# A planned dense stage is planned anew: other durations, a shared port between two engines, new priorities, and one DRAIN

## The chip, the core and the metric

The kernel runs on one core of a Trainium2 chip. A core has five engines with instruction queues of their own, each executed in order: TensorE (PE in the profile; PEld is its weight load), VectorE (DVE), ScalarE (ACT), GpSimd (POOL) and SyncE (SP), which issues most of the DMAs. They wait for each other by semaphores. The metric is the time of one execution on the device, in microseconds (us).

## The reference

Three layers over 4608 tokens (8 sequences of 576, 8 heads of 64). Everything is float32.

```python
kv = einsum('bhsd,bhse->bhde', k, v); out = einsum('bhsd,bhde->bhse', q, kv)
x = out / sqrt(mean(out*out, -1) + 1e-6) * g_norm            # attention without softmax; x is [4608, 512]

h = x @ w_in                                                 # dense layer: [512, 2048]
x = (h * clip(h + 3, 0, 6) / 6) @ w_out                      # [2048, 512]

out = x.copy()                                               # experts
xc = x[x @ w_skip > 0]; logits = xc @ w_gate                 # 8 experts, one for each token
e_idx = argmax(logits, 1); gate_w = softmax(logits)[e_idx]
y[mask_e] = gate_w * (maximum(xc[mask_e] @ w1[e], 0) @ w2[e])    # w1 [512, 1024], w2 [1024, 512]
out[x @ w_skip > 0] = xc + y
```

## The kernel before

**Products.** Every large product is made of three: each operand is split into a high part (rounded to the fp32r type) and a low part (what is left), and high x high, high x low and low x high are added in PSUM. Each split is a copy on ScalarE and a subtraction on VectorE or GpSimd.

**Dense stage.** Attention goes by 16 units `u` of 288 tokens and 4 head pairs `p`: `K` (k by v, fp32, from a load `kv` of 512 KB and one of 64 KB), `K2` and `K2m` (a mask on its result, VectorE), `A` (q by kv), `A2` (square), `B` (sum over a head), `B2l`, `B2`, `N`, `N2a`, `N2b`, `N2` (the norm), `Xh` and `Xl` (the split of x, which is the dense layer's input). The dense layer goes by 18 chunks `c` of 256 tokens and 16 blocks `f` of 128 of the 2048 columns: `G1` (12 matmuls into the PSUM tile `h`), `g` 1 to 4 (relu, product `t`, high part `gh`, low part `gl`), `G2` (6 matmuls into `y`). `route` then computes nine dot products a 128-token tile (`dot`), picks the expert and scatters the token's number into the table `tab` by an indirect DMA of GpSimd.

**Weights.** w_in and w_out come as 64-bit floats. `convert` turns each of 32 pieces (512 columns on 128 partitions; even numbers from w_in, odd ones from w_out) into float32 and splits it: `c1` to `c4` on VectorE (lines 600, 604, 607, 611), `sg` (line 615, a sum) on either engine, `h` on ScalarE, `l` (line 621, the low part) on either engine. Four staging places `SG` are used in turn. Chunks 0 and 1 are computed while the weights are being converted.

**What sets the order.** All these are `op`s: name, engine, a duration in us, the function that emits it, what it depends on, and tokens for buffers that it takes and gives. `Plan.order` goes through them as a list scheduler: at each moment every free engine takes the ready op with the highest priority (the longest chain behind it plus `BIAS` of its `kind`), and engine `VP` means VectorE or GpSimd, whichever takes it first, 2.05 times as long on GpSimd. The instructions are then emitted in the order of the planned starts. On the chip each engine goes through its list in order and waits where a dependency is late.

**Experts.** After the dense stage come 8 blocks of experts, written out by hand (`block`, `V128`), with side work in 10 steps of each block (`sd[0]` to `sd[9]`). GpSimd gathers the rows of an expert's tokens (`rows<-y_scr,idx`) and scatters the results (`final<-rows,idx`) by indirect DMAs. The next expert's counts are loaded in step 6 (`begin`); the last expert has none to load.

Of the kernel before, what the change touches and what calls it, by code (L numbers as in the profile page):

```python
# [28 lines left out]
    "t": 1, "g": 3, "row": 4, "rt": 2,  # L29
}  # L30
BIAS = {
# [11 lines left out]
    ("scat", 0): -250, ("scat", 1): -64, ("slot", 0): 104, ("slot", 1): -17, ("y", 0): -52, ("y", 1): -175,  # L43
    ("yd", 0): -90, ("yd", 1): 12, "bump": -172, "bump2": -190, "cp": -23, "fT": -185, "fTh": -7, "fTl": -165,
    "ixc": -50, "late h": 112, "late l": -40, "rowsc": -110, "wh": 14, "wl": -248, "wlo": 41, "z": -31,
    "zero": 250,
}
BIG = 1.0e6


class Plan:

# [11 lines left out]
    @staticmethod  # L64
    def kind(name):
        if isinstance(name, str):
            return name
        k, n = name[0], name[1]
        if k == "c":
            return ("ld" if name[2] == "ld" else "c", n // 8)  # L70
        if k in ("kv", "K", "K2", "K2m", "K2h"):
            return (k[0:1] if k[0] == "K" else k, min(n // 4, 2) + (n >= 12))
        if k[0] in "ABNX" or k in ("q", "qh", "ql"):
            return (k if k[0] == "q" else "A" if k[0] == "B" else k[0], min(n, 3) + (n >= 6))
        if k == "g":
            return ("g", name[3] + 4 * (n > 1) + 4 * (n > 3))
        if k in ("G1", "G2"):
            return (k, min(n, 2) + (n >= 4))
        if k in ("dot", "pick", "exp", "rank", "slot", "scat"):
            return (k, int(n >= 8))  # L80
        if k in ("y", "yd"):
            return (k, int(n >= 4))
        return k

    def add(self, name, eng, cost, fn, deps=(), take=(), give=(), dma=0.0, bonus=0.0):
        self.ops.append((name, eng, cost, fn, tuple(deps), tuple(take), tuple(give), dma, bonus))

    def order(self):
        ops = self.ops
# [21 lines left out]
        left = [len(p) for p in preds]  # L111
        done, start = {}, {}
        wait = {e: [] for e in self.ENGINES}
        giving, t, dma_free, n_left = [], 0.0, 0.0, len(ops)

        def add_wait(i):
            eng = ops[i][1]
# [10 lines left out]
        while n_left:  # L128
            keep, nxt = [], []
            for g in giving:  # L130
                if g[0] <= t + 1e-9:
                    self.free[g[1]] += 1
                else:
                    keep.append(g)
                    nxt.append(g[0])
            giving = keep
            for e in self.ENGINES:
                if busy[e] > t + 1e-9:
                    nxt.append(busy[e])
                    continue  # L140
                best = None
                for w in wait[e]:
                    if w[1] in start:
                        continue
                    if w[2] > t + 1e-9:
                        nxt.append(w[2])
                    elif best is None or w < best:
                        take = ops[w[1]][5]
                        if all(self.free[k] >= take.count(k) for k in take):
                            best = w  # L150
                if best is None:
                    continue
                i = best[1]
                _, eng, cost, _, _, take, give, dma, _ = ops[i]
                wait[e] = [w for w in wait[e] if w[1] not in start and w[1] != i]
                for k in take:
                    self.free[k] -= 1
                start[i] = t
                fin = busy[e] = t + (cost * 2.05 if eng == "VP" and e == "P" else cost)
                if e == "S":  # L160
                    dma_free = max(fin + self.DMA_ISSUE, dma_free) + dma
                    fin = dma_free + self.DMA_LAT
                else:
                    fin += dma
                done[i] = (fin, e)
                giving += [(fin + self.LAT * (e != "-"), k) for k in give]
                nxt += [busy[e], fin, t + 1e-6 if e == "-" else fin]
                n_left -= 1
                for j in succs[i]:
                    left[j] -= 1  # L170
                    if not left[j]:
                        add_wait(j)
                        nxt.append(t + 1e-6)
            if n_left:
                nxt = [x for x in nxt if x > t + 1e-9]
                assert nxt, [o[0] for i, o in enumerate(ops) if i not in start and not left[i]]
                t = min(nxt)
# [5 lines left out]
def fused_kernel(ctx, tc, qT, kvm, kvr, gv, w_in, w_out, w9, w9t, w1, w2, cst, tokid, out):  # L183
# [107 lines left out]
    def st_K(j):  # L291
        def mm(_):
            t = kv_t.pop(j)
            if j < 4:
                ps = ps_h.tile([128, 128], F32, tag="h", name="kvp")
            else:
                ps = ps_o.tile([128, 128], F32, tag="o", name="kvp")
            for i in range(5):
                n = 128 if i < 4 else 64
                nc.tensor.matmul(ps, t[0:n, 0, i, :], t[0:n, 1, i, :], start=(i == 0), stop=(i == 4))  # L300
            kvp_t[j] = ps

        op(("K", j), "PE", 2.1 if j < 3 else 1.07, mm, [("kv", j)] + [("y", 1, 1)] * (j >= 8), take=[k_tok(j)], give=["kv"] if j >= 8 else [])

    def st_K2(j):
        def km0(_):
# [59 lines left out]
    def st_A(u, p):  # L366
# [20 lines left out]
        op(("A", u, p), "PE", 0.48 if u < 2 else 0.36, mm, deps, take=[a_tok(u, p)],  # L387
           give=["qs", "qs"] * (u >= 2) + ["kh"] * (u % 2) + ["kl"] * (u % 2 and u > 2))

    def st_A2(u, p):  # L390
# [23 lines left out]
    def st_B(u, p):  # L414
# [8 lines left out]
            m_t[u, p] = m  # L423

        if u < 3:
            op(("B", u, p), "PE", 0.48, mm, [("A2", u, p)], take=[b_tok(u, p)])
        else:
            op(("B", u, p), "PE", 0.24, mm, [("A2l", u, p)], take=[b_tok(u, p)], give=["ss", "ss"])

    def st_B2(u, p):  # L430
        def ln(_):
# [43 lines left out]
    def st_N2(u, p):  # L475
# [13 lines left out]
        op(("N2a", u, p), "V", 0.37, f1, [("N", u, p)], give=[b_tok(u, p)])  # L489
        op(("N2b", u, p), "V", 0.43, f2, [("N", u, p), "consts"], give=[a_tok(u, p)])  # L490
        op(("N2", u, p), "V", 0.37, f3, [("N2a", u, p), ("N2b", u, p)], give=["a"] if u >= 3 else [])

    def st_X(u, p):
        parts, done = [], 0
# [179 lines left out]
    def G1(c, f):  # L674
# [11 lines left out]
            deps.append("late l")  # L686
        if f == 0 and c >= 2:
            deps += [("G1", c - 1, 15)] if c > 2 else [("G1", 0, 15), ("G1", 1, 15)]
        op(("G1", c, f), "PE", 1.31, mm, deps, take=["h"], bonus=1.28)

    h_t = {}

    def G1e(c, f):
# [23 lines left out]
            g_t[c, f] = (gh, gl)  # L717

        tk = "a" if second else "t"
        op(("g", c, f, 1), "A", 0.36, relu, [("G1", c, f)], take=[tk])  # L720
        op(("g", c, f, 2), "V", 0.34, mul, [("g", c, f, 1)], give=["h"])
        op(("g", c, f, 3), "A", 0.31, high, [("g", c, f, 2)], take=["g"])
        op(("g", c, f, 4), "VP", 0.34, low, [("g", c, f, 3)], give=[tk])

    def G2(c, f):
        def mm(_):
# [8 lines left out]
            mm3([(y_t[c][i], (gh[:, t], gl[:, t]), (wh[:, f % 4, :], wl[:, f % 4, :])) for i, t in enumerate(ts)], f == 0, f == 15)  # L735

        deps = [("w", ("out", f // 4), f % 4), ("g", c, f, 4)] + ([("G2", c, f - 1)] if f else [])
        op(("G2", c, f), "PE", 1.29, mm, deps, take=[] if f else ["y", "oy" if c == 1 else "y"],
           give=["g"], bonus=1.28)

    ysb = {}
# [66 lines left out]
    def route(i):  # L808

        for j in range(9):  # L810
            op(("dot", i, j), "V", 0.62, lambda _, j=j: rt_dot(i, j, j + 1), [("y", i // 2, i % 2), "w9"] + ([("dot", i, j - 1)] if j else [("dot", i - 1, 8)] if i else []),
               take=["rt"] if j == 0 else [])
        op(("pick", i), "V", 0.7, lambda _: rt_pick(i), [("dot", i, 8), ("cp", 1), ("cp", 2), ("cp", 3)], give=["row"])
        op(("exp", i), "A", 0.25, lambda _: rt_exp(i), [("pick", i)])
# [338 lines left out]
    for k in range(NE):  # L1153
# [100 lines left out]
```

## Time and profile before

| what | value |
|---|---|
| median of 3 runs | 1327.14 us (1323.95 to 1329.03) |
| the profiled execution's own time | 1326.83 us |
| its span, first to last instruction | 1325.1 us |
| mean granted TensorE clock | 0.982 |
| busy share of the span | PE 95%, DVE 68%, ACT 46%, POOL 28% |

The span is what the trace covers; the execution's own time is 1.7 us longer. A busy share is a mean over stages that differ: the first 185 us (attention of the first tokens, conversion of the weights, chunks 0 and 1), the rest of the dense stage up to about 897 us, the experts up to about 1312 us, and the end. The granted clock is a share of 2.4 GHz; 0.5 is the lower of its two levels, 1.2 GHz. Busy time on VectorE and GpSimd runs from an instruction's start to its end and may hold time in which it was held up.

### The profile page before, as it was taken

The page shows a single profiled execution, that of the slowest core. Times are in us where ns is not written, and L with a number is a line of the kernel's source. Part 1 is how long each engine was busy: PE and PEld are TensorE (multiplying, and loading weights), DVE is VectorE, ACT ScalarE, POOL GpSimd, SP SyncE. Part 2 cuts the span into 40 slices and gives each one's busy share as a digit, 9 for nine tenths or more (in the row PEclk, how much of TensorE's full clock was granted, in tenths as well). Part 3 has the DMA queues.
Part 4 walks back from the last instruction along what each step waited for, and adds up shares of the span by engine and source line. Part 5 has one row for each costly group of instructions (what it writes and reads, how often), then busy time and mean ns, then how long its engine had stood idle before and what let it go on. Part 6 is the DMA issues. An engine that isn't in the chain of part 4 may idle for free. (4 is left out here: it accounts for less than half of the span.)

```text
span 1325.1 us, 22326 instructions
## 1 busy us (share of the span) xinstructions
PE 1254.8 (95%) x7857; PEld 1120.5 (85%) x7857; DVE 899.0 (68%) x2435; ACT 603.3 (46%) x1514; POOL 376.1 (28%) x399
## 2 busy tenths in 40 slices
PE   5787799999999999999999999999999999999995
PEld 4676688898888998989989999998988888889885
DVE  4999989758778458768667767677675266555431
ACT  2543354535654334555554554563353255344320
POOL 2756744414331013122122122130043122223111
PEclk9798999999999999999999999999999999999998
DMA  9333343202111201121121121100146055555300
GB/s 300 101 111 112 96 167 100 77 1 82 51 19 55 86 1 46 59 68 46 42 68 59 47 68 42 47 5 33 65 143 187 32 188 168 164 180 165 127 25 24
DMA packets 77632, 114.48 MB, mean 86 GB/s; under 512 B 17158, under 2 KB 38550, under 8 KB 77360
## 3 DMA queue, kind: packets, MB, share of 16 engines
q1 hardware_dynamic: 70944, 98.12, 23.6%
q0 software_dynamic: 6544, 14.58, 3.4%
q8 instruction: 73, 1.20, 0.4%
q14 instruction: 71, 0.58, 0.2%
HBM read 91.25 MB, written 26.05 MB: 89 GB/s over the span
## 5 line engine op out<-in xcount | busy, mean ns | idle before, releaser
L768 DVE CUSTOM_DVE_ANT_0 junk<-ysb,w9b 128x512 bf16<-128x512 f32 x306 | 226.2, 739 | 4.9 <-ACT ysb L747 2.3
L701 ACT ACTIVATE t<-h,half 128x256 f32<-128x256 f32 x288 | 136.2, 474 | 205.0 <-PE h L665 103.5
L716 POOL TENSOR_TENSOR gl<-t,gh 128x256 fp32r<-128x256 f32 x120 | 103.3, 861 | 317.6 <-ACT gh L710 214.0
L710 ACT ACTIVATE gh<-t 128x256 fp32r<-128x256 f32 x288 | 119.5, 415 | 156.5 <-DVE t L706 104.7
L706 DVE SCALAR_TENSOR_TENSOR t<-t,h 128x256 f32<-128x256 f32 x288 | 119.8, 417 | 73.6 <-ACT t L701 71.8
L656 PE MATMUL y<-wh,gh 128*128 128x512 f32 x400 | 131.4, 403 | 1.2 <-ACT gh L710 1.1
L656 PE MATMUL y<-wl,gh 128*128 128x512 f32 x400 | 128.0, 394 | 1.7 <-DVE wl L621 1.7
L656 PE MATMUL y<-wh,gl 128*128 128x512 f32 x400 | 126.8, 392 | 0.1
L656 PE MATMUL y<-WH,gh 128*128 128x512 f32 x384 | 126.2, 404 | 0.0
L656 PE MATMUL y<-WH,gl 128*128 128x512 f32 x384 | 121.6, 392 | 3.6 <-DVE gl L716 3.6
L716 DVE TENSOR_TENSOR gl<-t,gh 128x256 fp32r<-128x256 f32 x168 | 81.2, 484 | 63.4 <-PE y L656 31.8
L656 PE MATMUL y<-WL,gh 128*128 128x512 f32 x384 | 122.1, 394 | 0.0
L665 PE MATMUL h<-x12h,wh 128*128 128x256 f32 x576 | 94.7, 287 | 15.2 <-DVE t L706 13.2
L665 PEld LDWEIGHTS h<-x12h,wh 128*128 128x128 f32 x576 | 84.4, 190 | 26.8 <-DVE t L706 17.1
L958 DVE SCALAR_TENSOR_TENSOR gl<-h,gh 128x256 fp32r<-128x256 f32 x88 | 37.3, 423 | 98.6 <-ACT gh L957 96.3
L957 ACT ACTIVATE gh<-h 128x256 fp32r<-128x256 f32 x88 | 33.8, 384 | 143.9 <-PE h L665 127.7
L665 PE MATMUL h<-x12h,wl 128*128 128x256 f32 x576 | 93.5, 285 | 0.0
L665 PE MATMUL h<-x12l,wh 128*128 128x256 f32 x576 | 93.4, 285 | 0.0
L656 PEld LDWEIGHTS y<-wl,gh 128*128 128x128 f32 x400 | 75.5, 189 | 20.0 <-DVE wl L621 2.6
L656 PEld LDWEIGHTS y<-wh,gl 128*128 128x128 f32 x400 | 75.4, 189 | 17.7 <-DVE gl L716 0.6
L656 PEld LDWEIGHTS y<-WH,gl 128*128 128x128 f32 x384 | 72.4, 189 | 20.5 <-DVE gl L716 4.5
L656 PEld LDWEIGHTS y<-WL,gh 128*128 128x128 f32 x384 | 72.7, 189 | 16.5
(205 smaller groups left out, 2722.1 us busy)
## 6 DMA issues: line engine op xcount, KB each, us to landing
kv<-kvm SPq DMA_DIRECT2D x24, 512.0 KB
stgh<-w SPq DMA_DIRECT2D x22, 512.0 KB
stgl<-w SPq DMA_DIRECT2D x21, 512.0 KB
stg<-w SPq DMA_DIRECT2D x21, 512.0 KB
y_scr<-ysb SPq DMA_DIRECT2D x36, 256.0 KB
final<-ysb SPq DMA_DIRECT2D x36, 256.0 KB
SG<-w_in SPq DMA_DIRECT2D x16, 512.0 KB
SG<-w_out SPq DMA_DIRECT2D x16, 512.0 KB
```

What stands on the lines that cost most here:

```text
L656: nc.tensor.matmul(ps, st[a], mv[b], start=first and (a, b) == (0, 0) and all(p[0] is not ps for p in prods[:q]), stop=last and (a, b) == ...
L665: nc.tensor.matmul(ps, st[a], mv[b], start=first and (a, b) == (0, 0) and all(p[0] is not ps for p in prods[:q]), stop=last and (a, b) == ...
L701: nc.scalar.activation(t, h_t[c, f], ACTF.Relu, bias=half, scale=1.0 / 6.0)
L706: nc.vector.scalar_tensor_tensor(t, t, 1.0, h_t.pop((c, f)), op0=ALU.min, op1=ALU.mult)
L710: nc.scalar.activation(gh, g_t[c, f], ACTF.Copy)
L716: eng_of[e].tensor_tensor(gl, t, f32(gh), op=ALU.subtract)
L768: nc.vector.tensor_tensor_reduce(junk, ysb[i], W9["t"][:, j, :], 1.0, 0.0, ALU.mult, ALU.add, accum_out=lg[:, j:j + 1])
L957: nc.scalar.activation(gh, ps, ACTF.Relu)
L958: nc.vector.scalar_tensor_tensor(gl, ps, 0.0, f32(gh), op0=ALU.max, op1=ALU.subtract)
```

## The change

The planner gets other durations (G1 from 1.31 to 1.44 us, G2 from 1.29 to 1.385, and smaller ones of the same kind), finer kinds, and with them a new table BIAS of 154 priorities. In the planner, an instruction on GpSimd and one on VectorE of the kinds that `alone` names no longer run at the same time: the later one begins when the `port` is free. At the end, the last expert's step 6 gets a DRAIN of GpSimd.

```diff
@@ BIAS (one line of 17 each)
-    ("c", 0): 40, ("c", 1): 18, ("c", 2): -117, ("c", 3): -140, ("dot", 0): 140, ("dot", 1): 61,
+    ("c", 1): 48, ("c", 2): -83, ("c", 3): 54, ("c", 4): -439, ("c", 5): 36, ("c", 6): -97, ("c", 7): -179,
...
@@ kind
         if k == "c":
-            return ("ld" if name[2] == "ld" else "c", n // 8)
+            if name[2] == "ld":
+                return ("ld", n // 2 if n < 16 else n // 4 + 4)
+            return ("cl" if name[2] in ("sg", "l") else "c", n // 4)
...
+    @staticmethod
+    def alone(name, eng):
+        if eng == "VP":
+            return True
+        return eng == "V" and not (name[0] in ("K2", "K2m", "N2a", "N2b", "slot", "fTl") or (name[0] == "g" and name[3] == 2))
+
@@ order
-                fin = busy[e] = t + (cost * 2.05 if eng == "VP" and e == "P" else cost)
+                if eng == "VP" and e == "P":
+                    cost = 2.05 * cost + 0.07
+                begin = t
+                if e in ("V", "P") and self.alone(ops[i][0], eng):
+                    begin = max(t, port)
+                    port = begin + cost - (0.2 if e == "P" else 0)
+                fin = busy[e] = begin + cost
...
-        op(("G1", c, f), "PE", 1.31, mm, deps, take=["h"], bonus=1.28)
+        op(("G1", c, f), "PE", 1.44, mm, deps, take=["h"], bonus=1.28)
...
-        op(("G2", c, f), "PE", 1.29, mm, deps, take=[] if f else ["y", "oy" if c == 1 else "y"],
+        op(("G2", c, f), "PE", 1.385, mm, deps, take=[] if f else ["y", "oy" if c == 1 else "y"],
...
@@ the loop over experts
         if k + 1 < NE:
             sd[6].append(lambda: begin(k + 1))
+        else:
+            sd[6].append(nc.gpsimd.drain)
```

What the new plan emits differs from the first instruction on. The lines of the changed kernel are 22 or 24 higher: 622, 626, 629, 633 are c1 to c4 (before 600, 604, 607, 611), 637 and 643 the sum and the low part (615, 621), 322 is K (300), 398 A of the first two units (376), 441 B (419), 687 G1 (665). `sh` and `sl` are places in the weights' buffers that hold kv, q and the norm's tiles while the weights are not there yet.

SP, from its first instruction. Before (`kvm` and `kvr` are the loads of k and v, `cst` constants, `SG` a conversion's staging place):

```order
L272 DMA sh_107<-kvm 128x2x512
L273 DMA sh_107<-kvr 64x2x128
L272 DMA sh_108<-kvm 128x2x512
L273 DMA sh_108<-kvr 64x2x128
L272 DMA sh_109<-kvm 128x2x512
L273 DMA sh_109<-kvr 64x2x128
L1040 DMA sh_106<-cst 128x128
L285 DMA sl_110<-qT 128x288 x4
L272 DMA sh_106<-kvm 128x2x512
L273 DMA sh_106<-kvr 64x2x128
L1039 DMA sh_106<-cst 128x272
L637 DMA SG<-w_in 128x4x256
```

(ahead of these stand one more pair of kvm and kvr). With the change:

```order
L659 DMA SG<-w_in 128x4x256 x2
L659 DMA SG<-w_out 128x1024
L1062 DMA sh_106<-cst 128x128
L659 DMA SG<-w_out 128x1024
L307 DMA sl_110<-qT 128x288 x4
L1061 DMA sh_106<-cst 128x272
L294 DMA sh_106<-kvm 128x2x512
L295 DMA sh_106<-kvr 64x2x128
L294 DMA sh_107<-kvm 128x2x512
L295 DMA sh_107<-kvr 64x2x128
L294 DMA sh_108<-kvm 128x2x512
L295 DMA sh_108<-kvr 64x2x128
```

Four conversion loads now stand ahead of the first load of k and v; before, five such pairs, two loads of constants and four of q stood ahead of the first conversion load.

VectorE, from the fifth instruction on (four memsets stand ahead in both; `km` is K2, `sl<-o` and `sl<-m` are N2b and N2a, `x0l` and `x12l` the low parts of x). Before:

```order
L1041 CAST boR<-sh_106 128x128
L308 TENSOR_TENSOR km_165<-kvp,boR 128x128
L308 TENSOR_TENSOR km_167<-kvp,boR 128x128
L1043 TENSOR_SCALAR g_sb<-g_sb 128x1
L308 TENSOR_TENSOR km_188<-kvp,boR 128x128
L308 TENSOR_TENSOR km_194<-kvp,boR 128x128
L600 TENSOR_SCALAR wbits<-SG 128x512
L604 SCALAR_TENSOR_TENSOR wbits<-SG,wbits 128x512
L607 TENSOR_SCALAR SG<-wbits 128x512
L611 SCALAR_TENSOR_TENSOR SG<-SG 128x512
L615 TENSOR_TENSOR wbits<-wbits,SG 128x512
L600 TENSOR_SCALAR wbits<-SG 128x512
```

With the change:

```order
L622 TENSOR_SCALAR wbits<-SG 128x512
L626 SCALAR_TENSOR_TENSOR wbits<-SG,wbits 128x512
L629 TENSOR_SCALAR SG<-wbits 128x512
L622 TENSOR_SCALAR wbits<-SG 128x512
L633 SCALAR_TENSOR_TENSOR SG<-SG 128x512
L626 SCALAR_TENSOR_TENSOR wbits<-SG,wbits 128x512
L622 TENSOR_SCALAR wbits<-SG 128x512
L1063 CAST boR<-sh_106 128x128
L629 TENSOR_SCALAR SG<-wbits 128x512
L1065 TENSOR_SCALAR g_sb<-g_sb 128x1
L622 TENSOR_SCALAR wbits<-SG 128x512
L633 SCALAR_TENSOR_TENSOR SG<-SG 128x512
```

The first conversion stood behind the four K2, and now stands first. In the order of VectorE's instructions the first c1 is at place 11 before and 5 now, the last low part of a weight at 258 and 260.

TensorE, up to its first dense matmuls. Before, it began with four K (rows not shown), then:

```order
L376 MATMUL o_192<-sl_110,km_165 128x288
L376 MATMUL o_196<-sl_110,km_167 128x288
L376 MATMUL o_201<-sl_110,km_188 128x288
L376 MATMUL o<-sl_110,km_194 128x288
L419 MATMUL m<-sl_112,boR 128x288 x2
L376 MATMUL o_235<-sl_111,km_167 128x288
L376 MATMUL o_240<-sl_111,km_194 128x288
L419 MATMUL m<-sl_112,boR 128x288 x2
L376 MATMUL o<-sl_111,km_165 128x288
L300 MATMUL kvp<-sh_106 128x128 x5
L419 MATMUL m<-sl_112,boR 128x288 x2
L665 MATMUL h<-x0h,WH 128x256 x4
```

With the change, behind six K, six A and three B:

```order
L441 MATMUL m<-sl_112,boR 128x288 x2
L322 MATMUL kvp<-sh_108 128x128 x5
L398 MATMUL o<-sl_110,km_262 128x288
L322 MATMUL kvp<-sh_109 128x128 x5
L441 MATMUL m<-sl_112,boR 128x288
L398 MATMUL o<-sl_111,km_225 128x288
L441 MATMUL m<-sl_112,boR 128x288
L687 MATMUL h<-x0h,WH 128x256 x4
```

The first `h` stood behind five K and came before the A of unit 1's third pair; now it stands behind eight K, all eight A of units 0 and 1 and seven of their eight B. The low part of x that it needs is at place 38 of VectorE's order before and 96 now.

Over the whole dense stage the choice between VectorE and GpSimd moves 69 instructions to GpSimd, 44 of them the low parts `gl` (line 716): 120 of 288 on GpSimd before, 164 now.

## Rows read from the trace of the kernel before

**Rows 1.** The page, part 1: busy us (share of the span) xinstructions.

```profile
PE 1254.8 (95%) x7857; PEld 1120.5 (85%) x7857; DVE 899.0 (68%) x2435; ACT 603.3 (46%) x1514; POOL 376.1 (28%) x399
```

**Rows 2.** Table by stages: stretch, its length, busy us (xinstructions) by engine, PEclk, DMA share, GB/s.

```profile
0.00:18.50 18.50, 11.32 (x41) 9.39 (x42) 1.50 (x10) 1.28 (x1) 1.51 (x6) 1.00 0.86 269
36.00:185.00 149.00, 117.96 (x648) 99.86 (x646) 145.82 (x224) 64.56 (x157) 94.90 (x80) 0.90 0.34 100
245.00:897.00 652.00, 649.23 (x4203) 588.18 (x4202) 459.92 (x1471) 332.34 (x880) 158.35 (x190) 1.00 0.16 48
897.00:1312.00 415.00, 407.19 (x2560) 363.61 (x2558) 222.50 (x520) 162.56 (x358) 87.97 (x86) 1.00 0.37 119
```

**Rows 3.** Timeline, PE, 35 to 37 us: start, us, instruction.

```profile
36.06 0.85 PE L665 MATMUL h<-x0h,WH 128*128 128x256 f32 x4
```

**Rows 4.** Waits of PE, 36 to 185 us: total, times, longest us.

```profile
PE h L665 <- DVE t L706: 21.7, 16, 3.4
```

**Rows 5.** Timeline, DVE, 18.4 to 21.6 us.

```profile
18.54 0.42 DVE L600 TENSOR_SCALAR wbits<-SG 128x512 int32<-128x512 int32 x1
19.00 0.69 DVE L604 SCALAR_TENSOR_TENSOR wbits<-SG,wbits 128x512 int32<-128x512 int32 x1
```

**Rows 6.** Groups of DVE, 18.5 to 185 us: busy us, mean ns | idle before.

```profile
L604 DVE SCALAR_TENSOR_TENSOR wbits<-SG,wbits 128x512 int32<-128x512 int32 x32 | 31.7, 995 | 0.1
L611 DVE SCALAR_TENSOR_TENSOR SG<-SG 128x512 f32<-128x512 uint32 x32 | 29.7, 932 | 0.1
L607 DVE TENSOR_SCALAR SG<-wbits 128x512 int32<-128x512 int32 x32 | 25.2, 793 | 0.1
L600 DVE TENSOR_SCALAR wbits<-SG 128x512 int32<-128x512 int32 x32 | 18.7, 584 | 0.0
L482 DVE SCALAR_TENSOR_TENSOR sl<-o,g_sb,sl 128x288 f32<-128x288 f32 x12 | 5.9, 510 | 2.5 <-ACT sl L470 2.4
```

**Rows 7.** Timeline, DVE and POOL, 98 to 100.6 us.

```profile
98.62 1.66 POOL L615 TENSOR_TENSOR wbits<-wbits,SG 128x512 f32<-128x512 f32 x1 [0.63 <-DVE SG L611]
99.06 1.43 DVE L515 TENSOR_TENSOR x12l<-sl,x12h 128x192 fp32r<-128x192 f32 x1
```

**Rows 8.** Timeline, DVE, 181 to 187 us.

```profile
183.09 1.50 DVE L621 TENSOR_TENSOR wl<-wbits,wh 128x512 fp32r<-128x512 f32 x1 [0.28 <-ACT wh L618]
```

**Rows 9.** Timeline, POOL, 1288 to 1313 us.

```profile
1289.12 0.98 POOL L934 DMA_INDIRECT final<-rows,idx  x1 [21.96 <-DVE rows L933]
...
1312.64 1.01 POOL L934 DMA_INDIRECT final<-rows,idx  x1 [0.34 <-DVEq L1196]
```

**Rows 10.** Line 1250, the end of the program: min/median/max ns, first and last start us.

```profile
L1250 POOLq DRAIN  x3: 46/109/8646, 1315.6 to 1324.8; - x3
```

**Rows 11.** Timeline, SP and PE, 0 to 6 us.

```profile
0.75 0.69 SPq L272 DMA_DIRECT2D sh<-kvm  x1
5.05 1.22 PE L300 MATMUL kvp<-sh 128*128 128x128 f32 x4 [5.05 <-DMA sh<-kvm]
```

**Rows 12.** Table, 36 to 185 us, of instructions on tile h, then on tile y.

```profile
36.00:185.00 149.00, 64.04 (x408) 59.35 (x408) 12.94 (x33) 15.21 (x33) 0.90 0.34 100
36.00:185.00 149.00, 47.12 (x174) 33.10 (x174) 0.00 (x0) 0.00 (x0) 0.90 0.34 100
```

**Rows 13.** Groups of DVE and POOL, 245 to 897 us.

```profile
L716 DVE TENSOR_TENSOR gl<-t,gh 128x256 fp32r<-128x256 f32 x129 | 58.6, 454 | 57.2 <-PE y L656 31.8 <-ACT gh L710 25.4
L716 POOL TENSOR_TENSOR gl<-t,gh 128x256 fp32r<-128x256 f32 x79 | 64.8, 820 | 292.7 <-ACT gh L710 195.9 <-PE pr L838 60.7 <-issue 25.9
```

**Rows 14.** DMA issues of POOL's queue, indirect.

```profile
rows<-y_scr,idx POOLq DMA_INDIRECT x38
tab<-pay,slot POOLq DMA_INDIRECT x36
final<-rows,idx POOLq DMA_INDIRECT x26
```

More of the change, by code (lines that the diff above doesn't have):

```diff
@@ L31 @@
 BIAS = {
[11 rows of a table removed]
[L43 to L46, printed above, removed]
[9 rows of a table added]
+    ("cl", 7): 216, ("dot", 0): -165, ("dot", 1): -278, ("exp", 0): 197, ("exp", 1): 139, ("g", 1): 195,
[6 rows of a table added]
+    ("ql", 3): -174, ("ql", 4): 62, ("rank", 0): 182, ("rank", 1): -20, ("scat", 0): 110, ("scat", 1): -260,
+    ("slot", 0): -206, ("slot", 1): -57, ("y", 0): 118, ("y", 1): -153, ("yd", 0): -155, ("yd", 1): -97,
+    "bo": 100, "bump": 200, "bump2": 189, "consts": -44, "cp": 10, "cs": -161, "cs1": -84, "fT": 234, "fTh": -118,
+    "fTl": 232, "g": -240, "ixc": 201, "late h": -33, "late l": 136, "rowsc": 101, "swap": -23, "tab": -241,
+    "tok": -95, "w": 98, "w9": 37, "wh": -287, "wl": -132, "wlo": 202, "z": -116, "zero": -26,
 }
@@ L69, in kind @@
         if k == "c":
-            return ("ld" if name[2] == "ld" else "c", n // 8)
+            if name[2] == "ld":
+                return ("ld", n // 2 if n < 16 else n // 4 + 4)
+            return ("cl" if name[2] in ("sg", "l") else "c", n // 4)
         if k in ("kv", "K", "K2", "K2m", "K2h"):
-            return (k[0:1] if k[0] == "K" else k, min(n // 4, 2) + (n >= 12))
+            return (k, min(n // 4, 2) + (n >= 12))
         if k[0] in "ABNX" or k in ("q", "qh", "ql"):
-            return (k if k[0] == "q" else "A" if k[0] == "B" else k[0], min(n, 3) + (n >= 6))
+            return (k if k in ("q", "qh", "ql", "A2l", "Xl") else "A" if k[0] == "B" else k[0], min(n, 3) + (n >= 6))
         if k == "g":
@@ L113, in order @@
         wait = {e: [] for e in self.ENGINES}
-        giving, t, dma_free, n_left = [], 0.0, 0.0, len(ops)
+        giving, t, dma_free, port, n_left = [], 0.0, 0.0, 0.0, len(ops)
         def add_wait(i):
@@ L301, in mm @@
             kvp_t[j] = ps
-        op(("K", j), "PE", 2.1 if j < 3 else 1.07, mm, [("kv", j)] + [("y", 1, 1)] * (j >= 8), take=[k_tok(j)], give=["kv"] if j >= 8 else [])
+        op(("K", j), "PE", 2.1 if j < 3 else 1.12, mm, [("kv", j)] + [("y", 1, 1)] * (j >= 8), take=[k_tok(j)], give=["kv"] if j >= 8 else [])
     def st_K2(j):
@@ L386, in st_A @@
             deps.append(("G1", u * UN // CH - 3, 15))
-        op(("A", u, p), "PE", 0.48 if u < 2 else 0.36, mm, deps, take=[a_tok(u, p)],
+        op(("A", u, p), "PE", 0.52 if u < 2 else 0.4, mm, deps, take=[a_tok(u, p)],
            give=["qs", "qs"] * (u >= 2) + ["kh"] * (u % 2) + ["kl"] * (u % 2 and u > 2))
@@ L425, in st_B @@
         if u < 3:
-            op(("B", u, p), "PE", 0.48, mm, [("A2", u, p)], take=[b_tok(u, p)])
+            op(("B", u, p), "PE", 0.5, mm, [("A2", u, p)], take=[b_tok(u, p)])
         else:
-            op(("B", u, p), "PE", 0.24, mm, [("A2l", u, p)], take=[b_tok(u, p)], give=["ss", "ss"])
+            op(("B", u, p), "PE", 0.27, mm, [("A2l", u, p)], take=[b_tok(u, p)], give=["ss", "ss"])
     def st_B2(u, p):
@@ L487, in f3 @@
             r_t[u, p] = r
-        op(("N2a", u, p), "V", 0.37, f1, [("N", u, p)], give=[b_tok(u, p)])
-        op(("N2b", u, p), "V", 0.43, f2, [("N", u, p), "consts"], give=[a_tok(u, p)])
-        op(("N2", u, p), "V", 0.37, f3, [("N2a", u, p), ("N2b", u, p)], give=["a"] if u >= 3 else [])
+        op(("N2a", u, p), "V", 0.4, f1, [("N", u, p)], give=[b_tok(u, p)])
+        op(("N2b", u, p), "V", 0.4, f2, [("N", u, p), "consts"], give=[a_tok(u, p)])
+        op(("N2", u, p), "V", 0.4, f3, [("N2a", u, p), ("N2b", u, p)], give=["a"] if u >= 3 else [])
     def st_X(u, p):
@@ L719, in G1e @@
         tk = "a" if second else "t"
-        op(("g", c, f, 1), "A", 0.36, relu, [("G1", c, f)], take=[tk])
-        op(("g", c, f, 2), "V", 0.34, mul, [("g", c, f, 1)], give=["h"])
-        op(("g", c, f, 3), "A", 0.31, high, [("g", c, f, 2)], take=["g"])
+        op(("g", c, f, 1), "A", 0.385, relu, [("G1", c, f)], take=[tk])
+        op(("g", c, f, 2), "V", 0.334, mul, [("g", c, f, 1)], give=["h"])
+        op(("g", c, f, 3), "A", 0.33, high, [("g", c, f, 2)], take=["g"])
         op(("g", c, f, 4), "VP", 0.34, low, [("g", c, f, 3)], give=[tk])
@@ L810, in route @@
         for j in range(9):
-            op(("dot", i, j), "V", 0.62, lambda _, j=j: rt_dot(i, j, j + 1), [("y", i // 2, i % 2), "w9"] + ([("dot", i, j - 1)] if j else [("dot", i - 1, 8)] if i else []),
+            op(("dot", i, j), "V", 0.69, lambda _, j=j: rt_dot(i, j, j + 1), [("y", i // 2, i % 2), "w9"] + ([("dot", i, j - 1)] if j else [("dot", i - 1, 8)] if i else []),
                take=["rt"] if j == 0 else [])
```

24 rows, old and new, of the table BIAS are left out of this document.

## The prediction

> **What bounds the kernel now.** I read the totals first: TensorE is busy 95% of the span [rows 1], so only its idle time can be won. The table by stages says where that lies [rows 2]. From 245 to 897 us TensorE idles 652.0 - 649.2 = 2.8 us, in the expert stage 415.0 - 407.2 = 7.8 us. What is left is the beginning and the end: from 36 us (the first matmul of the dense layer, 36.06 us [rows 3]) to 185 us TensorE works 118.0 of 149 us at a mean granted clock of 0.90, before that it has little to do, and in the last 14 us it does nothing.
>
> In the beginning the reader is to see VectorE: 145.8 of 149 us busy, GpSimd 94.9 us. TensorE's main wait there is for the tile t, a VectorE product (21.7 us in 16 waits [rows 4]). VectorE is late because it converts w_in and w_out: 32 conversions of four instructions each (c1 to c4) and two subtractions or sums (c5, low) that either engine takes. Alone, c1 takes 0.42 and c2 0.69 us [rows 5]; c3 and c4 are the same two kinds on the same 128x512 tile, so 2.22 us for a conversion. In the stage their means are 0.584, 0.995, 0.793 and 0.932 us, 105.3 us in all against 32 x 2.22 = 71.0 us alone: 34 us of VectorE's "busy" time is waiting [rows 6]. For whom, the timeline shows: a GpSimd sum runs from 98.62 to 100.28 us, and a VectorE subtraction of 192 columns that starts at 99.06 us ends at 100.49 us [rows 7], 1.43 us for 192 columns, where c2 takes 0.69 for 512. An instruction that reads PSUM (L482, mean 0.510 us) shows no such stretch [rows 6]. So what ends this stage is the two engines' work taken one after the other, and it begins when VectorE begins to convert, at 18.54 us [rows 5], and ends with the last low, 183.09 + 1.50 = 184.6 us [rows 8].
>
> At the end, the last scatter is issued at 1312.64 us [rows 9], and a DRAIN of GpSimd that begins at 1315.6 us takes 8.646 us of the 12.5 us that are left; the shortest DRAIN of that line took 0.046 us [rows 10].
>
> **The change, part by part.** The sum is made against the profiled execution, 1326.8 us, which is 0.3 us under the median of 1327.14.
>
> *The start of the conversions.* SP now issues two loads of w_in before anything else, then w_out; the kv loads come after four conversion loads, four of q and two of constants. Before, the first 512 KB load was issued at 0.75 us and its user ran at 5.05 us, 4.3 us later [rows 11]. By the same 4.3 us the first conversion can start at 5.1 instead of 18.54 us: 13.4 us earlier. What stands on VectorE from the first conversion to the last low is nearly the same: places 11 to 258 of its order before, 5 to 260 now, with 32 of each of c1 to c4 and 10 sums on VectorE in both; 9 subtractions before the last one then, 10 now; GpSimd has 22 sums and 22 subtractions, now 22 and 21. The eight more places are the six small instructions (boR, four km, g_sb) that stood ahead of the first conversion, and two others. Before, 247 places took 183.09 - 18.54 = 164.6 us, 0.666 us each, waits included. Now 255 places would take 170 us: the last low starts at 175 us and ends at 176.5, 8 us earlier. Counted by work alone (the six small ones take some 1.5 us, not 4) it would end at 5.1 + 164.6 + 1.5 + 1.5 = 172.7 us, 12 us earlier. Waits for the delayed kv are in the way: up to the first kv 3.5 MB stand in the queue, at the 269 GB/s of the first 18.5 us [rows 2] that is 13 us, and the four K took TensorE's 11.3 us of work up to 18.5 us. VectorE comes to its first km (place 20) at 15 us, so a wait of 1 to 3 us. I take 10 us. Bounds: nothing (all given back to waits), and 25 us, if the 34 us of waiting [rows 6] shrink by a third as well.
>
> *What comes after.* At the last low both orders have as much of chunks 0 and 1 behind them (14 and 14 second matmuls then, 15 and 15 now), and chunk 2 has just begun. From 245 us on TensorE is full [rows 2], so what is won in the beginning stays won, unless waits take it back there.
>
> *TensorE begins later.* The first matmul of chunk 0 now needs the fourth head pair's x, whose last part stands at place 96 of VectorE's order: 5.1 + 91 x 0.666 + 2 = 68 us instead of 36. The stage's matmuls into h and y are 64.0 + 47.1 = 111 us busy at clock 0.90 [rows 12], about 100 at the full clock that the next stages show. 68 + 100 to 111 = 168 to 179 us: with 10 to 11 conversions in stock TensorE can run without gaps, and would end about with VectorE. So this costs nothing as long as TensorE works nearly all the time.
>
> *More subtractions on GpSimd.* In the whole dense stage 44 of the 288 gl (128x256) move to GpSimd (120 before, 164 now). From 245 to 897 us one takes 0.820 us there and 0.454 us on VectorE [rows 13]. GpSimd is busy 158.4 of 652 us there, VectorE 459.9 [rows 2], and TensorE waits 2.8 us for everything: I take nothing. If that cover were gone, 44 x 0.366 = 16 us. The GPSIMD Engine Reference of the Trainium skill (4.1, Engine selection) speaks against this part: an elementwise operation with two inputs belongs on VectorE, GpSimd takes about twice the time. The rows agree (0.820 / 0.454 = 1.8); by that rule alone the forecast would be 16 us longer, 1325 us.
>
> *The other edits of the planner* (durations, finer kinds) act through the order alone. The end of the dense stage (first experts' weights, the first gather) is planned nearly as before; taken at nothing, with 3 us to either side.
>
> *The DRAIN.* In the last expert GpSimd gets one more DRAIN, behind the scatters of the expert before and ahead of its own. There GpSimd waits 21.96 us for VectorE before the scatter at 1289.12 us [rows 9], so 8.65 us more are hidden, and nothing else is queued behind it. What it does to the last DRAIN no row shows. Lower bound: it removes nothing, the long one stays. Upper bound: the last one becomes as short as the shortest, 8.6 us. Before the long one GpSimd had issued 38 + 36 + 26 indirect transfers [rows 14] and five plain ones; after the new one there are six first and last of six in [rows 9]. If a DRAIN's time goes with what was issued since the last one, the last would take 8.65 x 6 / 105 = 0.5 us. I take 8 us, since the two DRAINs that follow closely on the long one are the nearest rows, and they are short.
>
> Sum: 1326.8 - 10 - 8 = **1309 us**.
>
> **The rivals.** *The drain does nothing*: 1326.8 - 10 = 1317. For it: no row has a DRAIN after few transfers. Against: all transfers had landed when it began, so it does not wait for data.
> *The earlier start is given back*: kv, and with it x, come later, VectorE stands behind them in its fixed order, and the last low comes at 183 to 186 us; with the drain 1319. For it: three of the four km stand between conversions.
> *Neither acts*: 1327.
> *Slower: TensorE carries its waits along.* Before, it needed 149 us from its first dense matmul to the last low, 31 of them idle. If it needs as much from 68 us on, the stage ends at 217 us: 1326.8 + 32 - 8 = 1351. It breaks even, without the drain, at 149 - 32 = 117 us, and is slower by more than 0.5% above 117 + 8 + 6.6 = 132. For it: weights for the last conversions still come one by one. Against: its waits are for t and weights that came late [rows 4], and 10 to 11 conversions are now in stock.
> *Better*: VectorE's waiting shrinks by a third too; 25 us, so 1294.
>
> **How the numbers follow.** 0.5% of 1327 (6.6 us) is about what can be told from no change. Chances: the forecast 0.46 (1300 to 1317), no drain 0.20 (1309 to 1323), given back 0.14 (1315 to 1325), neither 0.07, slower 0.06, better 0.07. Under 1320.5 lie the forecast, four fifths of the second, 0.6 of the third and the last: 0.46 + 0.16 + 0.085 + 0.07 = 0.775; slower than 1333.8: 0.06; between: 0.165. The range 1295 to 1324 leaves out the slower case, "neither", half of the best and tails: about 0.2.
>
> **What would show it.** The first conversion (c1) starts at 5 to 6 us on VectorE; the last low ends at 170 to 180 us; TensorE's first dense matmul at 60 to 70 us, and from there to the last low over 90% busy with a granted clock near 1; from 245 us on less than 6 us idle per 650; a DRAIN of several us in the last expert beside matmuls, and one under 1 us at the end. Wrong I would be if the first conversion starts after 10 us, if TensorE still waits 20 us for t, or if the last DRAIN keeps its 8.6 us.

## The result, and the profile after

The changed kernel takes 1296.66 us (median of 4 runs, 1295.91 to 1297.89) against 1326.74 us before: ratio 0.9775, 95% interval 0.9754 to 0.9796, so 30 us less. The forecast was 1309 us, 18 us less. The direction and both causes were right. The ramp (the time up to the last low part of a weight) gave 11.5 us where 10 was forecast; nearly as much again came behind it, where the forecast had put nothing.

The profiled execution after took 1297.89 us, its span 1296.1 us, 29.0 us less than the span before. Its totals, the page's part 1 (as [rows 1]):

```profile
PE 1239.7 (96%) x7857; PEld 1113.4 (86%) x7857; DVE 897.5 (69%) x2366; ACT 603.9 (47%) x1514; POOL 437.8 (34%) x468
```

TensorE has as many instructions in 15.1 us less busy time. 69 instructions have moved from VectorE to GpSimd, and GpSimd's busy time is 61.7 us longer. Where the time went shows in the table by stages (as [rows 2], cut at the new ends):

```profile
0.00:18.50 18.50, 4.09 (x16) 3.65 (x17) 13.20 (x23) 2.54 (x3) 8.81 (x11) 1.00 0.93 300
36.00:173.00 137.00, 113.99 (x662) 99.32 (x662) 129.28 (x207) 64.18 (x157) 89.52 (x75) 0.91 0.33 97
173.00:185.00 12.00, 12.00 (x78) 10.88 (x77) 5.20 (x14) 6.00 (x14) 1.68 (x3) 1.00 0.93 332
185.00:245.00 60.00, 60.00 (x385) 54.06 (x384) 51.45 (x155) 31.41 (x86) 22.79 (x27) 1.00 0.18 56
245.00:868.00 623.00, 622.76 (x4064) 565.23 (x4063) 459.49 (x1430) 325.42 (x869) 205.74 (x246) 1.00 0.17 52
868.00:1290.00 422.00, 412.70 (x2601) 369.59 (x2600) 225.14 (x511) 164.87 (x363) 100.95 (x100) 1.00 0.36 117
```

VectorE works in the first 18.5 us, where it had 1.50 us of work before, and TensorE has no gap at all from 173 to 245 us. The timeline of VectorE names the first conversion (start, us, instruction; as [rows 5]):

```profile
5.49 0.43 DVE L622 TENSOR_SCALAR wbits<-SG 128x512 int32<-128x512 int32 x1 [4.39 <-DMA SG<-w_in]
```

and two lines (count, min/median/max ns, first and last start in us) name the last low part (as [rows 8]) and the last `t` of the dense stage:

```profile
L643 DVE TENSOR_TENSOR wl<-wbits,wh x5: 692/1354/1777, 118.4 to 172.4; 128x512 fp32r<-128x512 f32 x5
L728 DVE SCALAR_TENSOR_TENSOR t<-t,h x288: 403/417/880, 64.8 to 965.5; 128x256 f32<-128x256 f32 x144
```

The last low starts at 172.4 us and takes the line's minimum, 0.69 us: it ends at 173.1 us against 184.6. Before, the line of `t` reads:

```profile
L706 DVE SCALAR_TENSOR_TENSOR t<-t,h x288: 404/421/423, 52.6 to 989.0; 128x256 f32<-128x256 f32 x144
```

So the last `t` of the dense stage starts at 989.0 us before and 965.5 after. (The boundary at 897 us in the sections above lies inside the dense stage; the two stretches beside it are to be read so.) TensorE's waits from 36 to 185 us after (total, times, longest us; as [rows 4]):

```profile
PE m L441 <- ACT sl L415: 7.7, 2, 7.4
PE kvp L322 <- DVE sl L500: 5.1, 1, 5.1
PE h L687 <- POOL wl L643: 3.6, 3, 2.0
PE h L687 <- DVE t L728: 2.7, 3, 1.5
```

The wait for `t` has fallen from 21.7 to 2.7 us. The two long ones that are new stand before the first dense matmul (58.73 us on the timeline). It comes 22.7 us later than before; the first K starts at 14.4 us in place of 5.05. VectorE's conversion groups, 5 to 173.5 us (as [rows 6]), are c4, c2, c1, c3:

```profile
L633 DVE SCALAR_TENSOR_TENSOR SG<-SG 128x512 f32<-128x512 uint32 x32 | 30.5, 970 | 0.0
L626 DVE SCALAR_TENSOR_TENSOR wbits<-SG,wbits 128x512 int32<-128x512 int32 x32 | 27.4, 867 | 0.1
L622 DVE TENSOR_SCALAR wbits<-SG 128x512 int32<-128x512 int32 x32 | 21.6, 684 | 4.6 <-DMA SG<-w_in 4.6
L629 DVE TENSOR_SCALAR SG<-wbits 128x512 int32<-128x512 int32 x32 | 20.8, 665 | 0.1
```

That is 100.3 us against 105.3: only 5 of the 34 us of waiting inside them are gone. These means are still 0.18 to 0.28 us above the 0.42 and 0.69 us of one alone: the new order has not scheduled that waiting away. The page SBUF — State Buffer of the Trainium skill (SBUF: two separate sides) says that a VectorE operation in a two-port mode, or with two SBUF inputs beside a GpSimd operation that reads SBUF, contends with GpSimd for a shared pair of ports, and that the one that comes second fully blocks until the other is done. The longer means would fit that; no row here shows for each of them which engine it waited for.

The end, on GpSimd's timeline, the last scatter (as [rows 9]):

```profile
1290.64 1.01 POOL L956 DMA_INDIRECT final<-rows,idx  x1 [0.34 <-DVEq L1220]
```

and by lines (as [rows 10]) the new DRAIN of line 1005, an instruction ahead of the end, and the DRAINs there:

```profile
L1005 POOLq DRAIN  x1: 8156/8156/8156, 1249.3 to 1249.3; - x1
...
L1220 POOLq INC_SWDGE_SEM  x2: 318/1186/2054, 1218.8 to 1291.1; - x2
...
L1274 POOLq DRAIN  x3: 46/115/3170, 1291.6 to 1295.8; - x3
```

From the last scatter to the end of the span it was 1325.1 - 1312.64 = 12.4 us, now 1296.1 - 1290.64 = 5.5 us. So the 29.0 us divide into 22.0 us before the last scatter and 6.9 us behind it (rounded); 11.5 of the 22.0 us are there at the last low.

### The profile page after: what moved, and what is told of

It reads as the page before. It is cut to its first block, busy times and chain, and to the rows that moved or that the text cites. A ratio compares the mean times of both kernels' runs of the same rounds, so it can differ in the third digit from the quotient of the medians.

```text
span 1296.1 us, 22405 instructions
## 1 busy us (share of the span) xinstructions
PE 1239.7 (96%) x7857; PEld 1113.4 (86%) x7857; DVE 897.5 (69%) x2366; ACT 603.9 (47%) x1514; POOL 437.8 (34%) x468
## 5 line engine op out<-in xcount | busy, mean ns | idle before, releaser
L790 DVE CUSTOM_DVE_ANT_0 junk<-ysb,w9b 128x512 bf16<-128x512 f32 x306 | 249.3, 815 | 6.8 <-DMA w9b<-w 2.1
L738 POOL TENSOR_TENSOR gl<-t,gh 128x256 fp32r<-128x256 f32 x164 | 142.3, 868 | 327.0 <-ACT gh L732 218.2
L732 ACT ACTIVATE gh<-t 128x256 fp32r<-128x256 f32 x288 | 119.0, 414 | 173.5 <-DVE t L728 88.9
L728 DVE SCALAR_TENSOR_TENSOR t<-t,h 128x256 f32<-128x256 f32 x288 | 120.0, 418 | 59.3 <-ACT t L723 59.0
L738 DVE TENSOR_TENSOR gl<-t,gh 128x256 fp32r<-128x256 f32 x124 | 62.0, 500 | 76.2 <-PE y L678 47.9
L687 PEld LDWEIGHTS h<-x12h,wh 128*128 128x128 f32 x576 | 85.2, 189 | 15.1 <-issue 2.8
L956 POOL DMA_INDIRECT final<-rows,idx x26 | 26.2, 1007 | 201.4 <-DVE rows L955 198.3
```

The lines of the kernel that those rows point to most:

```text
L687: nc.tensor.matmul(ps, st[a], mv[b], start=first and (a, b) == (0, 0) and all(p[0] is not ps for p in prods[:q]), stop=last and (a, b) == ...
L728: nc.vector.scalar_tensor_tensor(t, t, 1.0, h_t.pop((c, f)), op0=ALU.min, op1=ALU.mult)
L732: nc.scalar.activation(gh, g_t[c, f], ACTF.Copy)
L738: eng_of[e].tensor_tensor(gl, t, f32(gh), op=ALU.subtract)
L790: nc.vector.tensor_tensor_reduce(junk, ysb[i], W9["t"][:, j, :], 1.0, 0.0, ALU.mult, ALU.add, accum_out=lg[:, j:j + 1])
L956: inst = nc.gpsimd.indirect_dma_start(out=out[:, :], out_offset=bass.IndirectOffsetOnAxis(ap=ix[:, t, 0:1], axis=0), in_=o, in_offset=None ...
```

## The experiments

Several of them don't plan at all but carry a written order: `ORDER` lists all 3999 ops of the dense stage with their engines, made from the lists that the two planners give, with every op behind what it depends on. Their diff is the same one line:

```diff
-    order = plan[0].order()
+    order = [(plan[0].ops[i // 8][3], ENG[i % 8]) for i in ORDER]
```

**The DRAIN alone.** The kernel before with

```diff
             sd[6].append(lambda: begin(k + 1))
+        else:
+            sd[6].append(nc.gpsimd.drain)
```

> The kernel before with the DRAIN in its last expert and nothing else. Theory (the tail is worth what the two traces show between the last scatter and the end, 12.4 us before and 5.5 after): 1326.7 - 7 = 1320 us, with a DRAIN of about 8 us inside the last expert, where GpSimd waits anyway, and a last one of about 3 us. Rival (a DRAIN takes as long at the end whatever stood before it, and the shorter tail comes from the other order): 1327 us and a last DRAIN of 8.6 us.

1319.68 us, ratio 0.9945 (0.9932 to 0.9958): -6.7 us, as the theory has it. The DRAIN inside and the last ones:

```profile
L983 POOLq DRAIN  x1: 8156/8156/8156, 1274.8 to 1274.8; - x1
...
L1252 POOLq DRAIN  x3: 46/115/2026, 1315.3 to 1318.4; - x3
```

**The kernel after without it** (the same two lines taken out).

> The kernel after without the DRAIN in its last expert. Theory (the DRAIN is worth the 7 us by which the two tails differ): 1296.7 + 7 = 1304 us, with a last DRAIN near 8.6 us. Rival (the tail is shorter for another reason): 1297 us.

1306.51 us, ratio to before 0.9848 (0.9831 to 0.9864): 9.8 us more than with it, above the 7 us expected. In the traces 6.9 us of it lie behind the last scatter (12.4 against 5.5 us) and 1.7 us ahead of it, where the order is the same in both kernels. The long DRAIN is back at the end, and so is the long instruction ahead of it:

```profile
L1218 POOLq INC_SWDGE_SEM  x2: 2053/2174/2294, 1220.5 to 1292.8; - x2
...
L1272 POOLq DRAIN  x3: 46/109/8646, 1295.3 to 1304.5; - x3
```

**A second DRAIN**, in the block behind the first one:

```diff
+            if k + 1 == NE:
+                sd[5].append(nc.gpsimd.drain)
             block(k, cur, 2, sd)
```

> The kernel after with a second DRAIN in the last expert, in the block that follows the first one, behind its two gathers and before its scatters. Theory (the last DRAIN takes what was issued since the one before it): the last DRAIN at or below 2.5 us instead of 3.17 us, about 1296 us, no measurable change of the time. Rival (what is left at the end is a fixed cost or the last scatter's own landing): 3.17 us again. If the second DRAIN delays the last scatters: above 1299 us.

```profile
L1005 POOLq DRAIN  x2: 3301/5728/8156, 1246.8 to 1270.5; - x2
...
L1276 POOLq DRAIN  x3: 46/115/3079, 1289.0 to 1293.3; - x3
```

1299.24 us, ratio 0.9793 (0.9779 to 0.9806), which the intervals don't tell from the kernel after. The second takes 3.30 us, and the last one is 3.08 us instead of 3.17: the rival. What is left at the end does not go with the number of transfers: two scatters are issued behind the second DRAIN, and six transfers behind the one DRAIN of the kernel after. It goes with the landing of the last scatter, which the trace gives from the scatter's start, here for this kernel and then for the kernel before with the DRAIN alone:

```profile
DMA to landing us min/median/max: 3.8/3.8/3.8
DMA to landing us min/median/max: 2.7/2.7/2.7
```

This kernel's last scatter starts at 1288.14 us and lands at 1292.0; the DRAIN ends at 1289.0 + 3.08 = 1292.1. With the DRAIN alone it starts at 1314.34 and lands at 1317.0; the DRAIN ends at 1315.3 + 2.03 = 1317.3. In the kernel after (1290.64, landing 3.8 us later) the two are 1294.5 and 1294.8. So the last DRAIN, with an earlier one before it, ends 0.1 to 0.3 us after the last scatter has landed, and takes 2.03 or 3.17 us as that landing comes. The long one at the end is something else: without the new DRAIN the last scatter lands at 1295.7 us, and the DRAIN runs on to 1303.9.

**The kv loads first again**, in the kernel after; SyncE's first places alone are changed, in the written order.

> The kernel after with the first loads of SyncE in the sequence of the kernel before: the four pairs for K, cs and the four q ahead of the four weight loads; the order of every other engine stays. Theory of the prediction (the earlier start of the conversions is the main term of the ramp): the first conversion back at 15 to 19 us, the last low part 10 to 13 us later, and 1296.7 + 10 to 13 = 1307 to 1310 us. Rival (the conversions have slack in the new order, or TensorE, which gets its first K some 9 us earlier, makes up for it): within 3 us of 1296.7.

1309.94 us, ratio to before 0.987 (0.9854 to 0.9886): 13.3 us more than the kernel after. The first conversion, the last low and the last `t`:

```profile
L622 DVE TENSOR_SCALAR wbits<-SG x6: 410/420/1500, 16.7 to 34.3; 128x512 int32<-128x512 int32 x6
...
L643 DVE TENSOR_TENSOR wl<-wbits,wh x6: 694/1156/1776, 128.3 to 183.0; 128x512 fp32r<-128x512 f32 x6
...
L728 DVE SCALAR_TENSOR_TENSOR t<-t,h x288: 402/416/424, 75.6 to 976.0; 128x256 f32<-128x256 f32 x144
```

In the new order each us by which the conversions begin later comes back almost whole: 11.2 us at the start, 10.6 at the last low, 10.5 at the last `t`. The rival, within 3 us of the kernel after, is refuted.

**The early start alone**: the new order up to the first G1, then the old.

> The order of the kernel after up to its first G1 only (the first 248 of 3999), then the order of the kernel before; no new DRAIN. The first conversion starts at 5.5 us as in the kernel after. Theory of the prediction (the earlier start is the whole gain of the ramp): the last low part at 172 to 176 us and 1315 to 1318 us. Rival (half of it comes from the order of the conversions themselves, where VectorE and GpSimd wait for each other less): the last low part near 179 us and about 1321 us.

1333.84 us, ratio 1.0064 (1.0051 to 1.0077): slower than before, beyond both theories. The first conversion starts at 5.3 us, yet the last low at 188.2 and the last `t` at 995.6 us:

```profile
L600 DVE TENSOR_SCALAR wbits<-SG x10: 412/422/1214, 5.3 to 40.0; 128x512 int32<-128x512 int32 x10
...
L621 DVE TENSOR_TENSOR wl<-wbits,wh x8: 680/1362/1782, 128.3 to 188.2; 128x512 fp32r<-128x512 f32 x8
...
L706 DVE SCALAR_TENSOR_TENSOR t<-t,h x288: 404/421/424, 70.6 to 995.6; 128x256 f32<-128x256 f32 x144
```

The table by stages of the same kernel, 60 to 100 us, and under it VectorE's longest wait there:

```profile
60.00:100.00 40.00, 35.68 (x209) 32.29 (x209) 23.02 (x51) 22.01 (x58) 15.00 (x20) 0.84 0.24 53
```

```profile
DVE t L706 <- ACT t L701: 10.4, 8, 4.3
```

VectorE works 23.0 of 40 us, and what it waits for is ScalarE's part of `t`, 10.4 us, while no wait for a load of weights is among its waits. The old order, in which TensorE begins at 36 us, lists products `t` of the first chunks ahead of the next conversions; with the first `t` at 70.6 instead of 52.6 us VectorE stands in front of them. The place where the two orders are joined takes part in this, so the 7 us are what the early start costs in front of the old order, and not in front of any order. In the kernel after the same stretch has it at work 39.2 us:

```profile
60.00:100.00 40.00, 38.69 (x239) 34.79 (x239) 39.19 (x73) 26.10 (x69) 27.41 (x27) 0.92 0.40 108
```

**The new order up to the last low, then the old; and the mirror image.**

> The kernel before, its dense stage in the order of the kernel after up to the op that ends the conversions (the first 732 of 3999), then all that is left in the order of the kernel before; no new DRAIN. Theory of the prediction (what the ramp wins stays won and nothing is added later): the last low part near 173 us, and 1326.7 - 11.5 = 1315 us. Second theory (TensorE has at that point also more of the chunks behind it, about 4 us of it): 1311 us. Rival (all that the dense stage won comes from its first 173 us, the rest of the order is worth nothing): -22, 1305 us.

> The mirror image: the order of the kernel before up to the op that ends the conversions (the first 729), then what is left in the order of the kernel after; no new DRAIN. The last low part stays at 184 us. If the order behind the ramp is worth something of its own (the two traces leave some 10 us for it): 1317 us. If it is worth nothing, as the prediction took it: 1327 us. If the new order only fits its own ramp: above 1328 us.

1320.49 us, ratio 0.9954 (0.9942 to 0.9967), and 1325.07 us, ratio 0.9992 (0.9982 to 1.0002): -5.9 and -1.3 us by the medians. The profiled execution of the first took 1316.08 us, the shortest of its five. The last `t`, the first kernel's row and then the second's:

```profile
L706 DVE SCALAR_TENSOR_TENSOR t<-t,h x288: 405/420/424, 64.1 to 979.2; 128x256 f32<-128x256 f32 x144
```

```profile
L706 DVE SCALAR_TENSOR_TENSOR t<-t,h x288: 403/418/423, 51.3 to 984.3; 128x256 f32<-128x256 f32 x144
```

Against 989.0 before, the traces give 9.8 us for the first part and 4.7 us for the rest, 14.5 together where the whole gives 23.5. By the medians the parts give 7.2 us, and the whole without its DRAIN 1326.7 - 1306.5 = 20.2. The halves don't add up. The first part is 13.3 us ahead at the last low (171.3 us) and loses 3.5 of them behind it. The rest is 1.3 us ahead at its last low (183.3 us), wins 3.4 us behind it, and loses 4.0 of its 4.7 us again in the experts, which I did not follow. The first kernel has the new ramp, but just behind it, from 173 to 185 us, TensorE works only 9.86 of 12 us, at clock 0.72, where the kernel after has 12.00 at 1.00:

```profile
173.00:185.00 12.00, 9.86 (x47) 8.82 (x48) 7.88 (x18) 7.52 (x21) 3.58 (x5) 0.72 0.56 206
```

**The new order to the end of chunk 2, then the old.**

> The order of the kernel after up to the last G2 of chunk 2 (the first 1052 of 3999), then what is left in the order of the kernel before; no new DRAIN. Theory (the whole gain of the dense stage is made in the conversions and in the chunk behind them, where the order must fit the state that the ramp leaves; chunks 3 to 17 are worth nothing): the last g2 of chunk 2 near 212 us, the end of the dense stage some 20 us before that of the kernel before, 1326.7 - 20 = 1306 us. Rival (the order of chunks 3 to 17 fits its own ramp too): 1310 to 1317 us, with TensorE idle between 245 and 400 us again.

1346.81 us, ratio 1.0146 (1.0131 to 1.0162): neither. From 245 to 300 us TensorE works 27 of 55 us, at clock 0.60; its largest wait from 240 to 300 us stands in the second block (behind it come 8.3 us for routing and 5.0 us for a `t`):

```profile
245.00:300.00 55.00, 26.96 (x127) 22.98 (x126) 27.57 (x117) 13.15 (x38) 7.63 (x10) 0.60 0.17 51
```

```profile
PE kvp L300 <- DMA kv<-kvm: 8.6, 2, 4.3
```

The new order does the attention of later units later than the old one does. What the old order had done by then now stands at the head of the rest in one lump: K 10 to 13, and loads, routing and A between them. So this cut measures its own seam, and the theory on chunks 3 to 17 is not tested by it.

**44 of the gl back on VectorE**, in the kernel after (the engine of 44 ops in the written order).

> The kernel after with 44 of the gl that its planner gave to GpSimd put back on VectorE, spread evenly over chunks 4 to 17 (121 are left on GpSimd, as many as in the kernel before); nothing else moves. Theory of the prediction (the gl lie under TensorE's work whichever engine does them): 1296.7 us, no change. Rival (GpSimd's gl are what lets VectorE keep up, part of the gain): above 1300 us. Other rival (each gl on GpSimd costs, 0.41 us more than one on VectorE): below 1294 us.

1298.98 us, ratio to before 0.98 (0.9781 to 0.982), 2.3 us more than the kernel after; the two intervals overlap (0.9754 to 0.9796 there), so they are not told apart. Neither rival, above 1300 or below 1294 us, came. From 245 to 868 us TensorE works 622.79 of 623 us, as with them on GpSimd (622.76).

**The planners without their tables, and the new one without the exclusion.**

```diff
-        prio = [rank[i] + self.bias.get(self.kind(o[0]), 0) for i, o in enumerate(ops)]
+        prio = [rank[i] for i, o in enumerate(ops)]
```

```diff
-                if e in ("V", "P") and self.alone(ops[i][0], eng):
+                if False:
```

> The planner of the kernel after (its durations, its exclusion, its kinds) with no table: priorities are ranks alone. The DRAIN stays. Theory (the new rules order better by themselves): shorter by 10 us and more than the planner of the kernel before without its table, the DRAIN's 7 us taken off. Rival (the table carries it): as long as that one within 10 us, both above 1340 us.

> The planner of the kernel before with no table. Theory (the table of the kernel before is worth tens of us): above 1340 us. Rival (the ranks alone give nearly the same order): within 10 us of 1326.7.

> The kernel after with its table and durations, but VectorE and GpSimd no longer exclude each other in the planner. Theory (table and rules belong together: any other rule makes another order, with late conversions or waits in the chunk behind them): 1305 to 1330 us. Rival (the exclusion does not matter to the order): within 4 us of 1296.7.

1572.14 us, 1539.53 us and 1366.99 us (ratios 1.1862, 1.1601 and 1.0298, each to within 0.003). The first misses its theory and its rival, the second bears out its theory, and the third lies 37 us above its theory's range. Without tables the new rules order worse than the old by 33 us, DRAIN included: the rules by themselves give nothing. With its table, and the exclusion alone gone, the new planner loses 70 us. TensorE then waits for `t` as before, from 36 to 960 us:

```profile
PE h L687 <- DVE t L728: 29.9, 35, 3.5
```

The table and the exclusion that it was made under act here as one thing; by these runs the gain can't be given to one of the edits of the planner. The new durations and the finer kinds were not taken out one by one.

## Why the prediction was right, and where its size was off

**The start of the conversions: right.** 5.1 us forecast, 5.49 measured; the last low 8 to 12 us earlier, 11.5 measured. Of the late kv, VectorE's first four `km` cost it 0.3 us in place of the 1 to 3 forecast; four waits for later K (line 335) cost 5.4 us more, where the same line cost 0.9 before. The last low came 11.5 us earlier all the same, in an order that was changed with the start: the early start alone gave back all of its lead and more, which is the rival "given back" at work, in the old order. The experiment with the kv loads shows the term by itself, 11 us in the trace.

**"What is won stays won": the step that failed.** The prediction put nothing behind the last low, though its own count had 28 G2 done there before and 30 now. From the last low to the last `t` it was 989.0 - 184.6 = 804.4 us, now 965.5 - 173.1 = 792.4: 12.0 us. The experts take 1.5 us back (323.6 us from the last `t` to the last scatter, now 325.1; TensorE idles 9.3 of 422 us where it idled 7.8 of 415 [rows 2]). So 10.5 of the 22.0 us come behind the last low. For the 12.0 us the rows tell three parts. First, TensorE is further on. At the last low it has done 421 matmuls into h and 180 into y from 36 us on, in 59.3 and 45.4 us, against 408 and 174 in 64.0 and 47.1 [rows 12]:

```profile
36.00:173.00 137.00, 59.28 (x421) 56.03 (x422) 13.70 (x34) 16.08 (x34) 0.91 0.33 97
36.00:173.00 137.00, 45.42 (x180) 33.07 (x180) 0.00 (x0) 0.00 (x0) 0.91 0.33 97
```

Into h one took 0.157 us in the ramp before and 0.141 after; from 245 to 868 us, at the full clock, it takes 0.132, into y 0.255. 13 and 6 matmuls more are worth 13 x 0.132 + 6 x 0.255 = 3.2 us; of A and B it has done five fewer, some 1 us, which leaves 2.2 us. Second, it idles no more: behind the last low it idled 60.0 - 58.3 = 1.7 us up to 245 us before,

```profile
185.00:245.00 60.00, 58.27 (x376) 51.80 (x377) 53.98 (x186) 32.39 (x92) 24.60 (x29) 1.00 0.40 130
```

and 2.8 us up to 897 us [rows 2]; after, 0.2 us up to 868: 4.3 us. The prediction saw the 2.8 us and left them where they were. Third, the weight loads into TensorE waited longer for `t` than its matmuls show as idle time. From the last low to the last `t`, before and after:

```profile
PEld h L665 <- DVE t L706: 4.8, 10, 1.0
PEld h L687 <- DVE t L728: 0.7, 1, 0.7
```

The matmuls' own waits for `t` there are 2.3 and 0.2 us. A matmul's end is modelled in the profile, so as an estimate (4.8 - 0.7) - (2.3 - 0.2) = 2.0 us of waiting stand inside what reads as busy. The remaining 3.5 us I could not trace to rows.

The two halves taken apart show that this gain belongs for the most part to the pair. From the last low to the last `t` the old order takes 804.4 us behind its own ramp and 807.9 behind the new one; the new order takes 801.0 us behind the old ramp and 792.4 behind its own.

**TensorE's late beginning: right in kind.** 68 us forecast, 58.73 measured, and no row shows a cost. From there to the last low TensorE is 91% busy at a mean granted clock of 0.95, where over 90% and a clock near 1 were forecast: 97% from 60 to 100 us, 87% from 100 to 173. The slower rival, with TensorE carrying 20 us and more of waits for `t`, did not come: 2.7 us.

**The gl on GpSimd: right, nothing.** The rival had 16 us for it; with 44 of them put back the time can't be told from the kernel after's, and TensorE is full from 245 to 868 us in either case. By the rule of the GPSIMD Engine Reference of the Trainium skill (4.1, Engine selection) such two-input operations belong on VectorE, being about twice as slow on GpSimd. The rows agree on the time of one [rows 13]; the 16 us by which the prediction would have lengthened its forecast for it did not come.

**The DRAIN: right in the sum, wrong in its working.** 8 us forecast; 6.9 in the traces, 6.7 alone, 9.8 by the medians as taken out. But the last one takes 3.17 us, not 0.5: it ends just after the last scatter has landed, a wait that the prediction's proportion to the transfers issued leaves out. The DRAIN itself so gives 5.5 us. The instruction ahead of it, INC_SWDGE_SEM, which the prediction had not counted, falls from 2.29 to 0.32 us, and the gap behind the DRAIN takes 0.5 us back. That the sum comes near 8 is in part luck.

**"Better", -25 us, by a third less waiting of VectorE,** gave nearly the measured time by another cause: that waiting shrank by 5 us, not 11. The measured 1296.7 us lie below the 1300 to 1317 of the forecast itself and 1.7 us above the lower end of the whole range, so the width of the range, and not the sum, took in the gain behind the last low.

## What to carry to other kernels

An early start is worth something only as far as the order behind it keeps the engine that sets the end at work; ask what it meets next in its queue, and when that is ready. When a stage's limiting engine is relieved, look also at what state the stage leaves to the next: how far the other engine has come, and the few us of idle time there. A planner's table is bound to the rules that it was made under: change both or none, and don't join halves of two orders. A DRAIN that must come at the end can be paid for, for the most part, where its engine waits anyway.

## What was not expected of the hardware

The first long DRAIN of GpSimd, with none before it but one at the very start, takes 8.156 us in the middle of the last expert, the same in three kernels, or 8.646 us at the end, long after the last transfer has landed. By its timeline GpSimd had issued 99 DMAs ahead of the one and 105 ahead of the other: 8.156 / 99 and 8.646 / 105 are both 0.0824 us. That fits the proportion that the prediction assumed, as far as two numbers can; no run varies the count further. A DRAIN behind that one takes 2.03 to 3.30 us and ends 0.1 to 0.3 us after the last transfer before it has landed, whether two transfers or six stand between them. The INC_SWDGE_SEM ahead of the last takes 2.29 us without an earlier DRAIN and 0.32 us with one; that line's other one, behind 92 DMAs, takes 2.05 us.
